# Early attention outputs split from PSUM into the first two token blocks, and token blocks cut at other places

## The chip, the core and the metric

The kernel runs on one core of a Trainium2 chip. TensorE (PE) multiplies matrices; PEld is its weight load. VectorE (DVE), ScalarE (ACT) and GpSimd (POOL) compute elementwise, and SyncE (SP) issues every transfer to or from DRAM. The engines run side by side, each takes its own instructions strictly in the program's order, and semaphores make one wait for another. The metric is the device time of one execution in microseconds.

## The reference

Causal attention with a decay bias, for 4 batches, 8 heads, 576 positions and 64 numbers a head; its output, reshaped to 2304 tokens of 512 numbers, passes through two MoE layers of width 2048. Everything is float32.

```python
scores = np.matmul(q, k.transpose(0, 1, 3, 2)) / np.sqrt(D)
cum = np.cumsum(np.maximum(s, 0.0), axis=-1)
bias = -(cum[:, :, :, None] - cum[:, :, None, :])
scores = np.where(causal, -1e9, scores + np.minimum(bias, 0.0))
attn = np.exp(scores - scores.max(-1, keepdims=True))
x = np.matmul(attn / (attn.sum(-1, keepdims=True) + 1e-09), v)
x = x.transpose(0, 2, 1, 3).reshape(B * S, H * D)
h = x @ w_in                      # first layer
x = (h * np.clip(h + 3.0, 0.0, 6.0) / 6.0) @ w_out
h = x @ w2_in                     # second layer; sp is log(1 + exp(h))
out = (h * np.tanh(sp)) @ w2_out
```

## The kernel before

**Products.** Every MoE operand is split into a high part, rounded to the multiplier's format, and a low part (value minus high part). A product is three matmuls: high by high, high by low, low by high. The split of a weight tile (`load_split`) is six instructions on ACT and DVE.

**Tokens.** The 256 early queries of each batch (`small`, two heads at a time: a pair) become tokens 0 to 1023; the 320 late queries of each batch (`unit`, also in pairs of heads) become tokens 1024 to 2303. `BLOCKS` cuts the tokens into five blocks. A block's tile `blk` holds, for each of 4 chunks of 128 channels, a high and a low part; chunk c comes from head pair c of every batch that the block covers. There are two such tiles (`"blk": 2`), reused in turn.

**MoE.** Each layer walks over the blocks, and in a block over 16 steps (`moe_step`). A step multiplies the 4 chunks by 128 columns of `w_in` (L730, three matmuls a chunk), applies the activation on ACT and DVE (L741, L743, L751), and multiplies by `w_out` (L763 in the first layer, L768 in the second).

**From attention to a block.** A pair's product with v (L683, PV below) is copied from PSUM to a staging tile `st`, stored to a DRAM tile `xs` (L689), and when all stores of a chunk have landed `load_block` loads it into the low half of `blk` (L711) and splits it: a high part (L288, ACT as a rule) and a subtraction (L369, DVE). Late units do the same through L577, L579 and L586. The layers' hand-over goes through `ys` likewise.

**The order.** All instructions are written into a list of nodes with costs, dependencies and priorities. `Plan.run` walks a model of the engines' time and emits each engine's instructions in the order in which the model starts them; the table `T` holds the costs and priorities that set it. Eight small pairs (batches 0 and 1, `FIRST`) come before the MoE; the other eight and the 16 late pairs (`WINDOWS`) are interleaved with the first layer's steps. While that lasts, attention uses two PSUM banks (`units(..., [6, 7], ...)`). `setup_b`, 32 rows for the cumulative sums, uses one `blk` tile first.

Of the kernel before, what the change touches and what calls it, by code (L numbers as in the profile page):

```python
# [10 lines left out]
F32 = mybir.dt.float32  # L11
F32R = mybir.dt.float32r
# [3 lines left out]
ALU = mybir.AluOpType  # L16

NB, NH, S, D = 4, 8, 576, 64
DM, DFF = 512, 2048
P = 128  # L20
NCC = DM // P
NF = DFF // P
NT = NB * S
BLOCKS = [(0, 512), (512, 512), (1024, 256), (1280, 512), (1792, 512)]
NBLK = len(BLOCKS)
# [6 lines left out]
CTOT = sum(CW)  # L32

T = dict(
    sm=4.004, sm2=3.667, w0=5.919, w1=9.193, cum=14.045, wo=1.212, blk0=27.645, blk1=17.49, wo2=34.767,
    wo2r=10.468, win2=5.088, g=13.066, upre=6.773, uhalf=0.799, upost=2.212, uv=0.453, spre=6.03, shalf=0.713,
    spost=1.762, pe=4.858, bias=2.981, la=1, la2=1, wp=5.083, p0=-20.0, p1=2.0, p2=2.856,
    p3=60.483, p4=82.61, p5=145.751, s0=28.447, s1=22.0, s2=22.848, s3=32.154, s4=71.114, s5=32.684,
)
# [27 lines left out]
class Plan:  # L67
# [56 lines left out]
    def run(self):  # L124
# [16 lines left out]
        now = 0.0  # L141
# [81 lines left out]
def v1x(n):  # L223
    return 0.069 + 0.00104 * n
# [19 lines left out]
def tile_attention_moe_moe(ctx, tc, qk1, qk, v1, s, w_in, w_out, w2_in, w2_out, out):  # L244
    nc = tc.nc

    def r(ap):
        return ap.bitcast(F32)
# [34 lines left out]
    def dyn(name):  # L283
        return lambda: pools[name]

    def copy(e, out_, in_):
        if e == "ACT":
            nc.scalar.activation(out=out_, in_=in_, func=AF.Copy)  # L288
        elif e == "POOL":
            nc.gpsimd.tensor_copy(out=out_, in_=in_)  # L290
        else:
            nc.vector.tensor_copy(out=out_, in_=in_)

    setup_b = Buf(main_p, "blk", [P, NCC, 2, 512], F32)

    def rows():
        room = setup_b.t.rearrange("p c a n -> p (c a n)")[0:NB * NH]
        s_sb, one, cum = (room[:, S * i:S * (i + 1)] for i in range(3))
        return s_sb, one, cum, room[:, 3 * S:3 * S + CTOT]
# [114 lines left out]
    class Pair:  # L414
        pass

    xs_n = {(i, c): [] for i in range(NBLK) for c in range(NCC)}
    all_att = []
# [171 lines left out]
    def small(b, h, pair, prio, step, dep0, depc, banks, fi, n_c1, n_id):  # L590
# [66 lines left out]
        n_r = A("DVE", 0.285, recip, n_exp, prio, (), [l])  # L657
        x = Buf(main_p, "st", [P, 512], F32)
        prev_t, n_p = None, []
# [20 lines left out]
        def pv():  # L680
            for g in range(2):
                for c, a in ((0, 0), (1, P)):
                    nc.tensor.matmul(out=po.t[D * g:D * (g + 1), a:N], lhsT=v.t[:, D * (2 * g + c):D * (2 * g + c + 1)], rhs=v.t[:, 4 * D + 384 * g + 2 * a:4 * D + 384 * g + 2 * a + N - a],  # L683
                                     start=c == 0, stop=c == 1)
        n_pv = A("PE", 0.73, pv, n_p + [n_v], post, [po, x], [v])
        pt_nodes.append(n_pv)
        n_x = A(("ACT", "DVE"), (actp(N), v1x(N)), lambda e: copy(e, x.t[:, 0:N], po.t[:, 0:N]), [n_pv], post, (), [po, x])
        i, o = divmod(token(b, 0), 512)
        xs_n[i, h // 2].append(A("SP", 0.5, lambda: nc.sync.dma_start(  # L689
            out=xs[i][h // 2][:, o:o + N], in_=x.t[:, 0:N]), [n_x], post, (), [x], lat=dma(P * N * 4)))  # L690

# [9 lines left out]

    blk, blk_n = {}, {}
    ys_n = {(i, c): [] for i in range(NBLK) for c in range(NCC)}
# [100 lines left out]
    with tc.manual_schedule():  # L804
# [6 lines left out]
        def open_pools():  # L811
# [35 lines left out]
        for n in range(tot):  # L847
            load_wo1(n, pos[n] - T["wo"], [n0])
        for i in range(NBLK):
            load_block(0, i, pos[NF * i] - T["blk0"])  # L850
# [80 lines left out]
```

## Time and profile before

| | us |
|---|---|
| median of three runs | 1023.62 (1021.73 to 1024.51) |
| the profiled execution's own time | 1021.91 |
| its span, first to last instruction | 1020.1 |
| PE busy in it | 988.0 (97%) |
| ACT, DVE busy | 523.1, 523.6 (51% each) |
| mean granted TensorE clock | 0.988 |

The profile is of one execution, 1.71 us below the median of the runs. PE's busy time counts overlapped matmuls once and is not work at full speed: an engine that waits inside a stretch at half clock shows as busy. The pace is read from the chain, where three 512-column matmuls take 0.68 us when they follow each other.

### The profile page before, as it was taken

Reading aid. Unit: us, or ns where it says so; the run is one execution under the profiler, and the core shown is the slowest. Engines: PE = TensorE matmul, PEld = TensorE weight load, DVE = VectorE, ACT = ScalarE, POOL = GpSimd, SP = SyncE. Lnnn points to the kernel's source line nnn. Section 1 sums busy time; section 2 is a strip of 40 time slices with the busy share of each in tenths; the row PEclk is TensorE's granted clock in tenths of the full one; section 3 lists DMA queues with packets and bytes.
Section 4 is the critical chain, followed back from the end, with each engine's and each line's share of the span. In section 5 each row is a group of like instructions: output and inputs, shape, how many; then the busy total and the mean of one; then the engine's idle time right before and its main releaser. Section 6 shows DMA issues by size and latency. Waiting matters only on the chain.

```text
span 1020.1 us, 14027 instructions
## 1 busy us (share of the span) xinstructions
PE 988.0 (97%) x5016; PEld 804.0 (79%) x5016; DVE 523.6 (51%) x1156; ACT 523.1 (51%) x1103; POOL 44.3 (4%) x102
## 2 busy tenths in 40 slices
PE   5789999999999999999999999999999999999998
PEld 3457777778778899978888888888888898888886
DVE  6778889986566666765628898311111212111111
ACT  5887878876655676665426456323222323223222
POOL 2101011200001000000000000000000000000000
PEclk9869999999999999999999999999999999999999
DMA  7778588885566486742646676001000201001001
GB/s 228 247 241 265 204 273 265 283 273 168 162 172 171 143 276 206 243 155 95 234 131 240 226 240 229 22 1 33 30 1 2 82 4 59 1 1 41 1 1 42
DMA packets 60357, 145.02 MB, mean 142 GB/s; under 512 B 6816, under 2 KB 21184, under 8 KB 60288
## 3 DMA queue, kind: packets, MB, share of 16 engines
q1 hardware_dynamic: 60288, 144.12, 43.6%
q8 instruction: 40, 0.66, 0.3%
q14 instruction: 29, 0.24, 0.1%
HBM read 121.32 MB, written 22.78 MB: 141 GB/s over the span
## 4 chain that ended last, share of the span: by engine, by line
PE 89%; ACT 6%; DVE 2%; DMA 2%; issue 1%; SPq 0%; DVEq 0%; ACTq 0%
PE b L730 37%; PE b L768 19%; PE b L763 19%; PE b L489 4%; PE b L573 3%; PE b L535 2%; PE b L628 2%; PE b L683 1%; ACT cb L524 1%; PE b L674 1%; DMA wraw<-in_w_out_dram 1%; ACT pt L288 1%; ACT cb L666 1%; ACT cb L647 1%; ACT wtmp L336 0%
## 5 line engine op out<-in xcount | busy, mean ns | idle before, releaser
L730 PE MATMUL b<-blk,win 128*128 128x512 f32 (+1 forms) x1920 | 498.3, 373 | 2.7 <-DVE blk L369 1.2
L730 PEld LDWEIGHTS b<-blk,win 128*128 128x128 f32 x1920 | 339.6, 189 | 70.0 <-issue 5.2
L763 PE MATMUL b<-g,wo 128*128 128x512 f32 (+1 forms) x960 | 259.7, 379 | 0.1
L763 PEld LDWEIGHTS b<-g,wo 128*128 128x128 f32 x960 | 164.7, 189 | 33.7 <-issue 8.6
L748 ACT ACTIVATE e<-b 128x512 f32<-128x512 f32 (+1 forms) x80 | 44.4, 554 | 254.5 <-PE b L730 254.4
L751 DVE TENSOR_TENSOR g<-e,g 128x512 fp32r<-128x512 f32 (+1 forms) x120 | 76.7, 639 | 173.4 <-ACT g L288 172.3
L768 PE MATMUL b<-wo,wo 128*128 128x512 f32 x432 | 121.1, 390 | 0.0
L768 PE MATMUL b<-wo,g 128*128 128x512 f32 x432 | 121.1, 390 | 0.0
L751 DVE TENSOR_TENSOR wo<-e,wo 128x512 fp32r<-128x512 f32 (+1 forms) x40 | 25.5, 638 | 140.4 <-ACT wo L288 140.3
L768 PEld LDWEIGHTS b<-wo,g 128*128 128x128 f32 x432 | 79.8, 188 | 15.5
L768 PEld LDWEIGHTS b<-wo,wo 128*128 128x128 f32 x432 | 79.8, 188 | 15.4
L741 ACT ACTIVATE e<-b,three 128x512 f32<-128x512 f32 (+1 forms) x80 | 51.2, 643 | 60.2 <-PE b L730 59.7
L288 ACT ACTIVATE g<-e 128x512 fp32r<-128x512 f32 (+1 forms) x108 | 64.1, 594 | 25.3 <-DVE e L743 17.4
L504 ACT ACTIVATE cb<-cb,nm 128x384 f32<-128x384 f32 (+2 forms) x80 | 54.6, 684 | 33.6 <-DVE nm L496 33.4
L743 DVE SCALAR_TENSOR_TENSOR e<-e,b 128x512 f32<-128x512 f32 (+1 forms) x80 | 50.4, 630 | 37.3 <-ACT e L741 36.4
L556 DVE TENSOR_TENSOR pt<-b,pt 128x384 fp32r<-128x384 f32 (+2 forms) x96 | 54.2, 576 | 23.6 <-ACT pt L288 22.4
L288 ACT ACTIVATE pt<-b 128x384 fp32r<-128x384 f32 (+2 forms) x96 | 47.9, 507 | 20.7 <-PE b L535 20.3
L496 DVE CUSTOM_DVE_ANT_0 cb<-b,cb 128x384 f32<-128x384 f32 (+2 forms) x80 | 44.7, 587 | 20.2 <-PE b L489 14.6
L535 PE MATMUL b<-ident,cb 128*128 128x128 f32 x304 | 48.9, 273 | 3.8 <-issue 2.7
L535 PEld LDWEIGHTS b<-ident,cb 128*128 128x128 f32 x304 | 37.3, 140 | 15.7 <-issue 5.6
L573 PEld LDWEIGHTS b<-pt,v 128*128 128x128 f32 x320 | 46.2, 189 | 3.2 <-ACT qk L288 1.2
L336 ACT ACTIVATE wtmp<-wraw 128x512 f32<-128x512 f32 x55 | 36.6, 665 | 23.6 <-DMA wraw<-in_w_out_dram 14.7
(79 smaller groups left out, 877.6 us busy)
## 6 DMA issues: line engine op xcount, KB each, us to landing
wo<-wos SPq DMA_DIRECT2D x64, 512.0 KB, 4.0
wraw<-in_w_in_dram SPq DMA_DIRECT2D x32, 512.0 KB, 4.2
wraw<-in_w_out_dram SPq DMA_DIRECT2D x32, 512.0 KB, 4.5
cb<-cuml SPq DMA_DIRECT2D x16, 896.0 KB, 6.8
wos<-wo SPq DMA_DIRECT2D x16, 512.0 KB, 6.8
qkr<-in_qk_dram SPq DMA_DIRECT2D x16, 480.0 KB, 5.0
qkr<-in_v_dram SPq DMA_DIRECT2D x16, 320.0 KB, 4.3
cb<-cums SPq DMA_DIRECT2D x12, 384.0 KB, 4.9
```

What stands on the lines that cost most here:

```text
L288: nc.scalar.activation(out=out_, in_=in_, func=AF.Copy)
L496: nc.vector.tensor_tensor_reduce(out=p.t[:, o:o + w], in0=pb.t[:, 0:w], in1=cb.t[:, o:o + w], scale=-0.125, scalar=(3.0e38 if a == 0 else ...
L504: nc.scalar.activation(out=p.t[:, o:o + w], in_=p.t[:, o:o + w], func=AF.Exp, scale=-1.0, bias=nm.t[:, k:k + 1], accum_out=l.t[:, k:k + 1],)
L535: nc.tensor.transpose(out=ps.t[:, P * z:P * (z + 1)], in_=p.t[:, o:o + P], identity=ident)
L556: nc.vector.tensor_tensor(out=dl, in0=s_, in1=r(dh), op=ALU.subtract)
L573: nc.tensor.matmul(out=po.t[:, a:nq], lhsT=w, rhs=pt.t[:, k, g, f:f + nq - a], start=c == 0 and k == 0, stop=c == tb - 1 and k == 1)
L730: nc.tensor.matmul(out=hps.t[:, 0:N], lhsT=w.t[:, a, P * c:P * (c + 1)], rhs=x.t[:, c, b, :], start=(c == 0 and k == 0), stop=(c == NCC - ...
L741: a = add("ACT", actp(N, 1), lambda: nc.scalar.activation(out=e0.t[:, 0:N], in_=hps.t[:, 0:N], func=AF.Relu, bias=three, scale=1.0), [prev ...
L743: a = add("DVE", v1x(N), lambda: nc.vector.scalar_tensor_tensor(out=e0.t[:, 0:N], in0=e0.t[:, 0:N], scalar=6.0, in1=hps.t[:, 0:N], op0=ALU ...
L751: gl = add("DVE", v1x(N), lambda: nc.vector.tensor_tensor(out=g.t[:, 1, 0:N], in0=src.t[:, 0:N], in1=r(g.t[:, 0, 0:N]), op=ALU.subtract), ...
L763: nc.tensor.matmul(out=y[j].t[:, 0:N], lhsT=wt.t[:, a, P * j:P * (j + 1)], rhs=g.t[:, b, 0:N], start=(f == 0 and k == 0), stop=(f == NF - ...
L768: nc.tensor.matmul(out=y[j].t, lhsT=g.t[:, a, P * j:P * (j + 1)], rhs=wt.t[:, b, :], start=(f == 0 and k == 0), stop=(f == NF - 1 and k == 2),
```

## The change

`small` writes its output straight into `blk`: the high part is copied from PSUM into `hl(0)`, the low part is subtracted from PSUM by DVE into `hl(1)`. The staging copy, the 16 stores and the 8 loads of the first two blocks are gone, with the 16 splits (8 high parts, 8 subtractions) behind the loads. The two tiles of blocks 0 and 1 are taken at the start, so `setup_b` moves to the attention pool's `pt` tile. Blocks 2, 3 and 4 are 384, 512 and 384 tokens in place of 256, 512 and 512. `Plan.run` multiplies PE's costs by 1.6 in its model's first 60 us, and most numbers of `T` are new.

```diff
-BLOCKS = [(0, 512), (512, 512), (1024, 256), (1280, 512), (1792, 512)]
+BLOCKS = [(0, 512), (512, 512), (1024, 384), (1408, 512), (1920, 384)]
...
-    p3=60.483, p4=82.61, p5=145.751, s0=28.447, s1=22.0, s2=22.848, s3=32.154, s4=71.114, s5=32.684,
+    p3=60.483, p4=83.372, p5=119.475, s0=31.523, s1=22.0, s2=23.277, s3=50.368, s4=66.006, s5=29.106,
...
+                    if e == "PE" and now < 60.0:
+                        c *= 1.6
...
-    setup_b = Buf(main_p, "blk", [P, NCC, 2, 512], F32)
+    setup_b = Buf(dyn("att"), "pt", [P, 3 * S + CTOT], F32)
...
-        x = Buf(main_p, "st", [P, 512], F32)
...
-        n_x = A(("ACT", "DVE"), (actp(N), v1x(N)), lambda e: copy(e, x.t[:, 0:N], po.t[:, 0:N]), [n_pv], post, (), [po, x])
         i, o = divmod(token(b, 0), 512)
-        xs_n[i, h // 2].append(A("SP", 0.5, lambda: nc.sync.dma_start(
-            out=xs[i][h // 2][:, o:o + N], in_=x.t[:, 0:N]), [n_x], post, (), [x], lat=dma(P * N * 4)))
+        c, xb = h // 2, blk[0, i]
+
+        def hl(k):
+            return xb.t[:, c, k, o:o + N]
+        n_xh = A(("ACT", "DVE"), (actp(N), v1x(N)), lambda e: copy(e, hl(0), po.t[:, 0:N]), [n_pv, blk_a[i]], post, (), [po, xb])
+        n_xl = A("DVE", v1x(N), lambda: nc.vector.tensor_tensor(
+            out=hl(1), in0=po.t[:, 0:N], in1=r(hl(0)), op=ALU.subtract), [n_xh], post, (), [po, xb])
+        blk_n[0, i, c] += [n_xh, n_xl]
...
+        for i in range(2):
+            blk[0, i] = Buf(main_p, "blk", [P, NCC, 2, 512], F32R)
+            blk_a[i] = add("X", 0.0, lambda: None, [n0], -1e6, [blk[0, i]])
...
-        for i in range(NBLK):
+        for i in range(2, NBLK):
             load_block(0, i, pos[NF * i] - T["blk0"])
```

The diff shifts the lines: L628, L674, L683, L730, L763 and L369 of before are L631, L676, L685, L736, L769 and L371 of the change, and the new subtraction is L695.

**The first MoE step on PE.** In a row b is a PSUM bank; L674 transposes the normalised scores, L628 makes scores. Before, the step's first chunk stands right behind the eighth pair's PV, and its second and third chunk together ten rows later:

```order
L730 MATMUL b_696<-blk,win 128x512 x3
L674 MATMUL b_713<-ident,cb 128x128 x3
L674 MATMUL b_720<-ident,cb 128x128 x3
L683 MATMUL b_738<-qk 64x256
L683 MATMUL b_738<-qk 64x128
L683 MATMUL b_738<-qk 64x256
L683 MATMUL b_738<-qk 64x128
L628 MATMUL b_746<-qkr 128x128
L628 MATMUL b_746<-qkr 128x256
L628 MATMUL b_756<-qkr 128x128
L628 MATMUL b_756<-qkr 128x256
L730 MATMUL b_696<-blk,win 128x512 x6
```

In the change, the rows that end with the step's fourth chunk are these. The step's first chunk stands ahead of the sixth pair's PV, the second ahead of the seventh's, and the third (in these rows) ahead of the eighth's:

```order
L631 MATMUL b_642<-qkr 128x128
L631 MATMUL b_642<-qkr 128x256
L676 MATMUL b_652<-ident,cb 128x128 x3
L676 MATMUL b_658<-ident,cb 128x128 x3
L736 MATMUL b_569<-blk,win 128x512 x3
L685 MATMUL b_674<-qk 64x256
L685 MATMUL b_674<-qk 64x128
L685 MATMUL b_674<-qk 64x256
L685 MATMUL b_674<-qk 64x128
L631 MATMUL b_687<-qkr 128x128
L631 MATMUL b_687<-qkr 128x256
L736 MATMUL b_569<-blk,win 128x512 x3
```

So the step's twelve matmuls, which before followed the eighth pair's PV with other work between them, now end behind that PV and half a pair of scores.

**SP's queue at the same place.** Before, stores (`xs<-st`) and loads (`blk<-xs`) stand among the loads of weights (`wraw`), inputs (`qkr`, `qk`) and bias rows (`cb`):

```order
L711 DMA blk<-xs_0_74 128x512
L608 DMA qk<-in_v_dram 128x2x128
L689 DMA xs_2_76<-st 128x256
L356 DMA wraw<-in_w_in_dram 128x512
L603 DMA qkr<-in_qk_dram 128x512
L605 DMA cb<-cums 128x768
L711 DMA blk<-xs_1_75 128x512
L608 DMA qk<-in_v_dram 128x2x128
L711 DMA blk<-xs_2_76 128x512
L689 DMA xs_3_77<-st 128x256
L356 DMA wraw<-in_w_in_dram 128x512
L605 DMA cb<-cums 128x768
```

In the change the queue holds only the latter:

```order
L611 DMA qk<-in_v_dram 128x2x128
L358 DMA wraw<-in_w_in_dram 128x512
L606 DMA qkr<-in_qk_dram 128x512
L611 DMA qk<-in_v_dram 128x2x128
L608 DMA cb<-cums 128x768
L606 DMA qkr<-in_qk_dram 128x512
L358 DMA wraw<-in_w_in_dram 128x512
L611 DMA qk<-in_v_dram 128x2x128
L358 DMA wraw<-in_w_in_dram 128x512
L611 DMA qk<-in_v_dram 128x2x128
L608 DMA cb<-cums 128x768
```

Four stores and four loads for block 0, and as many more stores beyond these rows, are gone from it.

**The start of block 2 on PE.** L573 is PV of a late pair, L535 its transposes. Before, the tenth late pair's PV stands between the first two chunks of block 2's first step; block 2 needs the first four late pairs only:

```order
L573 MATMUL b_3789<-pt,v 128x320 x6
L573 MATMUL b_3789<-pt,v 128x192 x2
L573 MATMUL b_3789<-pt,v 128x64 x2
L763 MATMUL b_2566<-g,wo 128x512 x3
L730 MATMUL b_3735<-blk,win 128x256 x3
L535 MATMUL b_3816<-ident,cb 128x128 x3
L763 MATMUL b_2578<-g,wo 128x512 x3
L535 MATMUL b_3828<-ident,cb 128x128 x3
L763 MATMUL b_2536<-g,wo 128x512 x3
L730 MATMUL b_3735<-blk,win 128x256 x3
L763 MATMUL b_2553<-g,wo 128x512 x3
```

In the change, with 384 tokens, block 2 needs late pairs of batches 0 and 1; the last of them is the ninth in the order, and its PV opens these rows (L576). The fourth chunk of block 2's first step stands 13 rows behind the last row here:

```order
L576 MATMUL b_3593<-pt,v 128x320 x6
L576 MATMUL b_3593<-pt,v 128x192 x2
L576 MATMUL b_3593<-pt,v 128x64 x2
L769 MATMUL b_2412<-g,wo 128x512 x3
L538 MATMUL b_3619<-ident,cb 128x128 x3
L769 MATMUL b_2432<-g,wo 128x512 x3
L736 MATMUL b_3631<-blk,win 128x384 x3
L769 MATMUL b_2445<-g,wo 128x512 x3
L538 MATMUL b_3645<-ident,cb 128x128 x3
L769 MATMUL b_2501<-g,wo 128x512 x3
L538 MATMUL b_3656<-ident,cb 128x128 x4
L736 MATMUL b_3631<-blk,win 128x384 x3
```

So the block's first chunk moved to four rows behind the PV of a pair from which its fourth chunk is made.

## Rows read from the trace of the kernel before

**Rows 1.** The page's first part, busy time of each engine.
```profile
PE 988.0 (97%) x5016; PEld 804.0 (79%) x5016; DVE 523.6 (51%) x1156; ACT 523.1 (51%) x1103; POOL 44.3 (4%) x102
```

**Rows 2.** Busy time (x instructions), granted clock, DMA by stretch; columns in the first row.
```profile
core 0: us, PE busy (x) PEld busy (x) DVE busy (x) ACT busy (x) POOL busy (x), PEclk, DMA share, GB/s
...
20.00:57.30 37.30, 26.44 (x150) 16.68 (x146) 27.51 (x109) 32.95 (x112) 5.56 (x10) 0.82 0.76 248
57.30:80.00 22.70, 19.31 (x77) 12.12 (x78) 18.51 (x52) 18.41 (x49) 2.97 (x6) 0.77 0.74 238
...
140.00:215.00 75.00, 72.42 (x384) 55.36 (x383) 69.29 (x160) 62.15 (x137) 8.81 (x14) 1.00 0.77 252
...
490.00:600.00 110.00, 110.00 (x487) 91.10 (x486) 76.18 (x128) 51.56 (x85) 0.00 (x0) 1.00 0.61 207
```

**Rows 3.** Timeline of PE and ACT: start, duration, line, work, idle time before it.
```profile
55.11 1.78 PE L683 MATMUL b<-qk 128*64 128x256 f32 x8
...
57.35 0.49 PE L730 MATMUL b<-blk,win 128*128 128x512 f32 x1 [0.46 <-ACT blk L288]
...
75.30 1.42 PE L730 MATMUL b<-blk,win 128*128 128x512 f32 x5 [0.77 <-DVE blk L369]
...
77.42 0.68 ACT L741 ACTIVATE e<-b,three 128x512 f32<-128x512 f32 x1
```

**Rows 4.** Timeline of SP, the store and the load of block 0's fourth chunk.
```profile
57.95 0.38 SPq L689 DMA_DIRECT2D xs<-st  x1
...
65.02 0.38 SPq L711 DMA_DIRECT2D blk<-xs  x1
```

**Rows 5.** PE's groups by shape, 57.3 to 80 us: count, busy us, mean ns, idle before.
```profile
L730 PE MATMUL b<-blk,win 128*128 128x512 f32 x23 | 8.7, 492 | 2.1 <-DVE blk L369 1.2 <-ACT blk L288 0.9
L674 PE MATMUL b<-ident,cb 128*128 128x128 f32 x18 | 4.3, 352 | 1.3 <-ACT win L288 0.7 <-ACT cb L666 0.4 <-issue 0.3
L628 PE MATMUL b<-qkr 64*128 64x256 f32 x10 | 3.4, 479 | 0.0
...
L683 PE MATMUL b<-qk 128*64 128x256 f32 x8 | 2.4, 533 | 0.0
```

**Rows 6.** Chain that ended last, three places: start, duration, work.
```profile
76.72 0.33 PE b L674 x3
...
80.52 0.85 PE b L628 x4
...
82.26 0.81 PE b L683 x8
...
259.54 0.69 PE b L763 x3
260.23 1.24 PE b L573 x10
261.47 0.77 PE b L763 x3
...
805.72 2.15 PE b L730 x18
```

**Rows 7.** DVE's groups by shape: count, busy us, mean ns.
```profile
L369 DVE TENSOR_TENSOR blk<-blk 128x512 fp32r<-128x512 f32 x32 | 21.7, 686 | 10.0 <-ACT blk L288 9.6
...
L556 DVE TENSOR_TENSOR pt<-b,pt 128x256 fp32r<-128x256 f32 x16 | 6.7, 418 | 0.2
```

**Rows 8.** The columns of rows 2 for a shorter stretch.
```profile
62.00:66.00 4.00, 4.00 (x16) 2.64 (x15) 1.87 (x6) 2.34 (x5) 0.00 (x0) 0.50 0.80 214
```

**Rows 9.** Timeline of DVE, a late pair's last add and the split behind it, twice.
```profile
438.06 0.49 DVE L579 TENSOR_TENSOR st<-b,st 64x320 f32<-64x320 f32 x1 [0.99 <-ACT st L577]
...
447.49 0.69 DVE L369 TENSOR_TENSOR blk<-blk 128x512 fp32r<-128x512 f32 x1
...
218.13 0.49 DVE L579 TENSOR_TENSOR st<-b,st 64x320 f32<-64x320 f32 x1
...
236.95 0.42 DVE L369 TENSOR_TENSOR blk<-blk 128x256 fp32r<-128x256 f32 x1
```

More of the change, by code (lines that the diff above doesn't have):

```diff
@@ L34 @@
 T = dict(
-    sm=4.004, sm2=3.667, w0=5.919, w1=9.193, cum=14.045, wo=1.212, blk0=27.645, blk1=17.49, wo2=34.767,
-    wo2r=10.468, win2=5.088, g=13.066, upre=6.773, uhalf=0.799, upost=2.212, uv=0.453, spre=6.03, shalf=0.713,
-    spost=1.762, pe=4.858, bias=2.981, la=1, la2=1, wp=5.083, p0=-20.0, p1=2.0, p2=2.856,
-    p3=60.483, p4=82.61, p5=145.751, s0=28.447, s1=22.0, s2=22.848, s3=32.154, s4=71.114, s5=32.684,
+    sm=4.004, sm2=3.667, w0=5.919, w1=9.193, cum=14.045, wo=0.795, blk0=27.645, blk1=17.49, wo2=40.913,
+    wo2r=11.978, win2=5.088, g=29.605, upre=6.511, uhalf=0.883, upost=2.212, uv=0.304, spre=9.559, shalf=0.728,
+    spost=1.761, pe=4.796, bias=2.278, la=1, la2=1, wp=5.083, p0=-8.796, p1=2.0, p2=2.856,
+    p3=60.483, p4=83.372, p5=119.475, s0=31.523, s1=22.0, s2=23.277, s3=50.368, s4=66.006, s5=29.106,
 )
@@ L292, in copy @@
             nc.vector.tensor_copy(out=out_, in_=in_)
-    setup_b = Buf(main_p, "blk", [P, NCC, 2, 512], F32)
+    setup_b = Buf(dyn("att"), "pt", [P, 3 * S + CTOT], F32)
     def rows():
-        room = setup_b.t.rearrange("p c a n -> p (c a n)")[0:NB * NH]
+        room = setup_b.t[0:NB * NH]
         s_sb, one, cum = (room[:, S * i:S * (i + 1)] for i in range(3))
@@ L415, in tile_attention_moe_moe @@
         pass
+    blk, blk_n, blk_a = {}, {}, {}
     xs_n = {(i, c): [] for i in range(NBLK) for c in range(NCC)}
@@ L684, in pv @@
                                      start=c == 0, stop=c == 1)
-        n_pv = A("PE", 0.73, pv, n_p + [n_v], post, [po, x], [v])
+        n_pv = A("PE", 0.73, pv, n_p + [n_v], post, [po], [v])
         pt_nodes.append(n_pv)
-        n_x = A(("ACT", "DVE"), (actp(N), v1x(N)), lambda e: copy(e, x.t[:, 0:N], po.t[:, 0:N]), [n_pv], post, (), [po, x])
         i, o = divmod(token(b, 0), 512)
-        xs_n[i, h // 2].append(A("SP", 0.5, lambda: nc.sync.dma_start(
-            out=xs[i][h // 2][:, o:o + N], in_=x.t[:, 0:N]), [n_x], post, (), [x], lat=dma(P * N * 4)))
+        c, xb = h // 2, blk[0, i]
[5 more added lines that the diff above has]
+        blk_n[0, i, c] += [n_xh, n_xl]
     def units(b, ta, tb, prio, step, n0, nc0, banks, fi=False, hs=(0, NH)):
@@ L700, in units @@
         all_att.extend(pl.nodes[n1:])
-    blk, blk_n = {}, {}
     ys_n = {(i, c): [] for i in range(NBLK) for c in range(NCC)}
@@ L825, in tile_attention_moe_moe @@
                   lat=dma(NB * NH * 1500 * 4))
+        for i in range(2):
+            blk[0, i] = Buf(main_p, "blk", [P, NCC, 2, 512], F32R)
+            blk_a[i] = add("X", 0.0, lambda: None, [n0], -1e6, [blk[0, i]])
+            for c in range(NCC):
+                blk_n[0, i, c] = []
         all8 = [6, 7, 4, 5, 0, 1, 2, 3]
```

## The prediction

> **What bounds the kernel now.** I read the page's first part, the busy times by stretch, the timeline around the first MoE step, the groups by shape, and the chain that ended last, in this order. PE is busy 97% of the span, ACT and DVE half of it [rows 1]. By stretch, PE is full from 80 us on: between 490 and 600 us it is busy for 110.00 of 110 us, and even from 140 to 215 us, where DVE is at 92%, it idles 2.6 of 75 us [rows 2]. So the matmuls are a floor that this change doesn't lower, and time can only come from what PE loses. It loses most at the start: from 20 to 57.3 us it is busy 26.44 of 37.3 us at a clock of 0.82, while ACT is at 88%; the small pairs are made there, and ACT and DVE set their pace.
>
> The place that the change touches is behind that. The eighth pair's PV ends at 56.9 us; the first step's first matmul starts at 57.35, its last two only at 75.30, and its activation at 77.42 [rows 3]. What the step waits for is the way through DRAM: the fourth chunk's store was issued at 57.95, its load at 65.02 [rows 4], and the matmuls at 75.30 waited for DVE's split of it [rows 3].
>
> What PE loses there comes from counting its work at full-clock pace. Between 57.3 and 80 us stand 23 MoE matmuls, 18 transposes, 10 wide scores (and 10 narrow) and 8 wide PVs (and 8 narrow) [rows 5]. In the chain three MoE matmuls take 0.69 us, three transposes 0.33, four score records 0.85, eight PV records 0.81 [rows 6]. That is 23 x 0.23 + 6 x 0.33 + 5 x 0.85 + 2 x 0.81 = 13.1 us. The stretch is 22.7 us long, so 9.6 us are lost, to waits and to the half clock that rows show from 62 to 66 us [rows 8].
>
> **The change, part by part.** The sum is made against the profiled execution's 1021.9 us; the runs' median lies 1.7 higher, and the forecast is given on the median's scale. Less than 0.3% (3.1 us) can't be told from no change here.
>
> *Until the eighth pair's output is split: +0.6.* In the order, DVE has 157 instructions up to that subtraction, where it had done 141 by 57.3 us: 8 subtractions, one more weight tile, some normalisations taken from ACT. ACT has 90 against 96. Ten more at the 0.42 us of a 256-column subtraction [rows 7] are 4.2 us; ACT and DVE together worked 60.5 us in the 37.3 us before [rows 2], 1.62 us per us, so 2.6 us later. By then PE has nine MoE matmuls behind it that it had not before, with the same scores, transposes and PVs: 9 x 0.23 = 2.0 earned. Bounds: -2.0 (DVE, idle a quarter of that stretch, hides all) to +2.1 (all ten instructions on the path). I take the joint pace, since ACT's 88% leaves little room.
>
> *The stretch behind it: -6.1.* The step then lacks only three matmuls, and up to the fourth step nothing but weight tiles that the order puts earlier. What stays lost in such a stretch: PE idles 2.6 in 75 us from 140 to 215 us [rows 2], so 0.7 in 20 us. A return from attention to the MoE costs 0.08 (three matmuls take 0.77 behind a PV, 0.69 otherwise [rows 6]), ten of them 0.8. And the clock: a stretch of 4 us at half [rows 8] costs 2.0; before, half clock lasted longer, but behind PE's pauses. 9.6 - 3.5 = 6.1. Bounds: 0 gained (ACT and DVE take the place of the wait) to 8.8 (only the returns stay).
>
> *More returns: +0.9.* The order has 215 returns from attention to the MoE, before 196. Without four ahead of the first step's end and ten in the stretch above, and six of before's until 80 us, it is 201 against 190: 11 x 0.08. The shortest gap taken, 0 is the other bound.
>
> *Block 2's last chunk: +0.5.* Block 2 now needs the ninth late pair, whose PV stands just ahead of it. From that PV to the block's fourth chunk the order has 24 MoE matmuls of 512 columns, 9 of 384, 19 transposes, one PV and six returns: 24 x 0.23 + 9 x 0.173 + 19 x 0.11 + 1.24 + 0.5 = 10.9 us of cover [rows 6]. What must fit in it is a copy and an add, a store, a load and a split. Seven late pairs between 350 and 490 us show that chain; in the middle one 9.6 us pass from the add's end (438.55) to the split's (448.18) [rows 9], and the copy and the add itself need some 1.1 before. So cover and chain are equal: usually no wait, now and then 1 or 2. Behind PE's wait stand all its matmuls. The longest case, at 218 us, took 18.8 us [rows 9], where nothing was in a hurry: 0 to 9 are the bounds, and 0.5 is near the lower since the seven are the nearer rows.
>
> The Trainium skill has a shorter chain: DMA: Bandwidth & Descriptors, section "Anatomy of one DMA", gives a transfer a fixed 2 us and its bytes at 436 GB/s. By that, estimated for a store of 32 KB and a load of 192 KB, the two take 4.6 us, the cover holds in every case, and the sum below would be 0.5 us lower. That section fits transfers issued from GpSimd; these are issued by SP, and here 8.9 us lie between the middle case's add and its split's start.
>
> *Blocks of 384: 0.* Both kernels have the same columns and matmuls. A 256-column matmul takes 2.15/18 = 0.119 us, a 512-column one 0.23 [rows 6]. On the line through both, two of 384 cost just what a 256 and a 512 do. In proportion to the 512 it would be -2.3 us over 576 triples, in proportion to the 256 +4.6; 384 is midway, so I take the line.
>
> *Hidden.* DVE's 16 subtractions of 256 columns instead of 8 of 512 cost 16 x 0.418 - 8 x 0.686 = 1.2 us more [rows 7], half of it counted above, the rest while PE is full. A pair's bank is held a subtraction longer, 8 x 0.42 = 3.3 us if every later pair stalled PE; the second bank covers it. SP issues 24 transfers less, and waits for nobody's pace in doing so. Block 1's tile is free from the start, but its first matmul stands 350 MoE matmuls behind. The sums' rows leave `pt` long before a late pair takes it. The first layer's last block is a quarter shorter, with the second layer's weights split beside it; DVE at 76.18 of 110 us there [rows 2] would rise to 92%: hidden, barely.
>
> Sum: 0.6 - 6.1 + 0.9 + 0.5 = -4.1, so 1017.8, and 1019.5 on the median's scale.
>
> **The rivals.**
> - *DVE takes the place of the wait.* It carries 57 instructions more than before in the whole program (ACT 57 fewer), and is at 92% from 140 to 215 us [rows 2]; if PE now waits for weight tiles and activations from 60 us on, the 6.1 are not gained: +2.0, 1025.6, no change. For it: the matmuls' floor leaves DVE less room when PE comes earlier. Against it: by the order, DVE's work up to the same step is no larger, and before it kept pace with a full PE.
> - *More than forecast.* The step comes while the clock is up, PE waits for nothing, and DVE's idle quarter hides its added work: -2.0 - 8.8 + 0.9 = -9.9, 1013.7. For it: the new order feeds PE MoE matmuls between the pairs, where it paused. Against: weights are still made by the same two engines.
> - *Slower: block 2's last chunk comes late.* The store stands in SP's in-order queue, the splits in ACT's and DVE's. With the chain of 218 us PE waits 18.8 + 1.1 - 10.9 = 9.0 us: -4.1 - 0.5 + 9.0 = +4.4, 1028.0. It makes the kernel slower by more than 0.3% from a chain of 18.4 us on. For it: the new place has no slack. Against: the seven nearer chains.
>
> That the transfers are not gone is no rival: the order shows SP's queue without them.
>
> **How the numbers follow.** The forecast (1016.5 to 1022) has 0.42, "more" 0.21, DVE 0.22, block 2 0.15. The time is the forecast's, 1019.5. Faster by over 0.3% is below 1020.5: seven tenths of the forecast and all of "more", 0.50. Slower is block 2 and a little of DVE's case, 0.17; the rest, 0.33, is within 0.3%. The range goes from 1012, below "more" with a 384-column gain, to 1027, past DVE's case and up to most of block 2's; some 0.15 is left out.
>
> **What would show it.** Right: the first activation starts near 62 us instead of 77.4; from there to 80 us PE loses 3 to 4 us against its work; no store or load of `xs` before the late pairs'; 384-column matmuls at 0.17 us; no wait above 1 us at block 2's fourth chunk. Wrong: the eighth pair's subtraction later than 63 us; PE waiting for `win`, `wo` or `g` between 60 and 215 us; a wait of several us for `blk` when the 384-column matmuls begin; or a wait where the second layer begins.

## The result, and the profile after

| | before | after |
|---|---|---|
| median (lowest to highest), us | 1023.66 (1021.73 to 1024.51) | 1013.81 (1013.02 to 1014.32) |
| the profiled execution, us | 1021.91 | 1013.87 |
| its span, us | 1020.1 | 1012.1 |

The ratio is 0.9902, 95% interval 0.9885 to 0.9919: faster, by 9.85 us, where 4.1 were forecast. The profiled executions differ by 8.0 us, since that of before lay 1.7 below its median; the stretches below are theirs.

The page's first line of the change, against [rows 1]: DVE has 57 instructions more, ACT 57 fewer, and PE the same 5016.

```profile
PE 992.1 (98%) x5016; PEld 826.6 (82%) x5016; DVE 541.8 (54%) x1213; ACT 496.0 (49%) x1046; POOL 45.0 (4%) x102
```

Busy time by stretch in the change, with the columns of [rows 2]:

```profile
20.00:57.30 37.30, 33.39 (x174) 20.01 (x171) 32.13 (x122) 32.80 (x107) 5.15 (x11) 0.91 0.69 217
57.30:80.00 22.70, 22.49 (x94) 15.24 (x95) 19.66 (x54) 16.64 (x45) 4.03 (x6) 0.85 0.71 221
140.00:215.00 75.00, 74.16 (x404) 58.49 (x403) 66.59 (x155) 55.21 (x125) 7.22 (x16) 1.00 0.78 247
490.00:600.00 110.00, 110.00 (x561) 100.54 (x560) 70.80 (x122) 49.55 (x85) 0.00 (x0) 1.00 0.61 208
...
58.50:65.20 6.70, 6.70 (x17) 4.17 (x16) 5.79 (x20) 4.94 (x15) 0.00 (x0) 0.50 0.59 182
```

From 20 to 57.3 us PE ran 174 matmuls where it had run 150, and it idled 0.8 us from 140 to 215 us in place of 2.6. It still ran at half clock from 58.5 to 65.2 us.

The change's timeline at the first step, to be read beside [rows 3]:

```profile
45.93 0.96 PE L736 MATMUL b<-blk,win 128*128 128x512 f32 x3
...
48.47 1.19 PE L736 MATMUL b<-blk,win 128*128 128x512 f32 x3
...
52.70 1.27 PE L736 MATMUL b<-blk,win 128*128 128x512 f32 x3 [0.40 <-ACT blk L290]
...
56.63 0.49 PE L736 MATMUL b<-blk,win 128*128 128x512 f32 x1 [0.72 <-ACT blk L290]
57.51 0.73 PE L736 MATMUL b<-blk,win 128*128 128x512 f32 x2 [0.39 <-DVE blk L695]
...
57.04 0.42 DVE L695 TENSOR_TENSOR blk<-b,blk 128x256 fp32r<-128x256 f32 x1
...
59.12 0.67 ACT L747 ACTIVATE e<-b,three 128x512 f32<-128x512 f32 x1
```

The four chunks are multiplied while the pairs are still being made, the last of them right behind its own subtraction, and the activation starts at 59.12 us in place of 77.42.

**Where the time went.** PE's busy time hides slow matmuls, so I count its work instead. Each matmul is given the time that it takes in an undisturbed run of its kind (0.227 us for 512 columns, 0.173 for 384, 0.119 for 256, 0.108 for a transpose; small scores and PVs by [rows 6], and so on). The whole program then is 940.7 us in every kernel here. Time passed minus the work that PE had started is *lost time*. What is lost in each stretch, in the profiled execution of every run of this study (the experiments below say what each run is):

| us lost | to 57.3 | 57.3 to 80 | 80 to 490 | 490 to end | sum |
|---|---|---|---|---|---|
| before | 29.0 | 10.4 | 35.2 | 4.7 | 79.3 |
| after | 26.9 | 5.6 | 29.9 | 9.0 | 71.3 |
| split_alone | 27.9 | 3.5 | 35.3 | 4.7 | 71.5 |
| no_split | 31.1 | 11.8 | 29.9 | 9.5 | 82.3 |
| old_blocks | 26.8 | 6.9 | 40.2 | 4.8 | 78.6 |
| no_factor | 32.4 | 3.2 | 36.3 | 9.0 | 81.0 |
| old_table | 28.4 | 2.8 | 33.3 | 9.0 | 73.5 |
| nudged | 26.3 | 6.2 | 33.0 | 9.0 | 74.4 |
| dve_twice | 27.2 | 7.8 | 31.3 | 8.9 | 75.3 |
| act_twice | 26.6 | 7.9 | 29.8 | 9.0 | 73.3 |
| split_factor | 28.0 | 2.6 | 35.2 | 4.8 | 70.5 |
| old_blocks_p5 | 26.8 | 7.0 | 27.9 | 4.7 | 66.4 |
| old_blocks_p5_163 | 26.6 | 5.7 | 28.5 | 4.7 | 65.5 |
| searched | 26.3 | 4.8 | 27.9 | 4.7 | 63.7 |
| no_split_p5 | 31.3 | 11.9 | 30.9 | 5.1 | 79.3 |
| no_factor_p5 | 31.2 | 4.3 | 34.9 | 4.7 | 75.0 |

Each row is one execution, and the executions of one kernel differ (no_factor took 1016.38 to 1024.08 us, and its profiled one 1023.54), so that a difference of a us between two rows says little.

From before to after: -2.1, -4.7, -5.4, +4.2, together -8.0 (worked out before rounding). The forecast had looked for its gain in the second column alone; what the last two columns hold, which nearly cancels, was not in it.

The rows of the third column's stretch, before and then after:

```profile
80.00:490.00 410.00, 404.26 (x2344) 329.69 (x2343) 295.48 (x685) 285.20 (x616) 31.16 (x72) 1.00 0.66 210
```

```profile
80.00:490.00 410.00, 407.56 (x2279) 336.52 (x2278) 309.45 (x717) 267.59 (x577) 30.76 (x73) 1.00 0.64 203
```

PE's open idle time fell from 5.7 to 2.4 us, and between these two kernels nearly all of that is one group of waits. PE's transposes of late pairs, 80 to 490 us, before and after (the last fields are idle time before them and what ended it):

```profile
L535 PE MATMUL b<-ident,cb 128*128 128x128 f32 x304 | 48.9, 273 | 3.8 <-issue 2.7 <-DVE pt L556 0.8
```

```profile
L538 PE MATMUL b<-ident,cb 128*128 128x128 f32 x304 | 48.7, 273 | 0.6 <-DVE pt L559 0.4
```

3.2 of the 5.4 us are here; the other 2.2 are in matmuls that follow each other more closely, and what closed them up is not shown. One such wait of before, in its timeline:

```profile
208.97 1.03 PE L535 MATMUL b<-ident,cb 128*128 128x128 f32 x8
...
209.17 0.63 ACT L288 ACTIVATE g<-e 128x512 fp32r<-128x512 f32 x1 [0.80 <-PE b L763]
209.71 1.06 ACT L288 ACTIVATE pt<-b 128x512 fp32r<-128x512 f32 x2
210.32 1.29 DVE L556 TENSOR_TENSOR pt<-b,pt 128x512 fp32r<-128x512 f32 x2 [0.22 <-ACT pt L288]
...
211.11 1.09 PE L535 MATMUL b<-ident,cb 128*128 128x128 f32 x5 [1.11 <-issue]
```

Eight transposes fill the two banks that attention has. Their copies out of PSUM stand on ACT behind a split of `g`, which waits for PE itself; PE goes on when they and DVE's subtractions have emptied the banks. Where such a knot falls is a matter of the written order.

The fourth column has two parts. The chain of the change in the second layer, in a block of 384 tokens (start, duration, work), and at the same place that of the run "split_alone", whose blocks are the old ones:

```profile
839.26 0.70 PE b L774 x3
839.96 0.53 PE b L736 x3
840.49 0.69 PE b L774 x3
841.18 0.52 PE b L736 x3
```

```profile
839.54 0.68 PE b L772 x3
840.22 0.68 PE b L734 x3
```

Three matmuls of 384 columns take 0.52 to 0.53 us, on the forecast's line or just above it; but three of 512 between them take 0.69 to 0.70 in place of 0.68. The kernel before has the same surcharge in its one block of 256 tokens, in its chain:

```profile
799.78 0.69 PE b L768 x3
800.47 0.35 PE b L730 x3
800.83 0.69 PE b L768 x3
```

The change has two blocks of 384 tokens, in place of that one and one of 512. From 490 to 1000 us it loses about 3 us more than before, nearly all of it in matmuls whose neighbours have another width. And at the end, in the timeline of before and then of the change:

```profile
1009.78 2.88 PE L768 MATMUL b<-wo,wo 128*128 128x512 f32 x12
```

```profile
1003.62 0.86 PE L774 MATMUL b<-wo,wo 128*128 128x512 f32 x3
1004.91 2.47 PE L774 MATMUL b<-wo,g 128*128 128x512 f32 x9 [0.44 <-ACT g L290]
```

Before, twelve matmuls stood behind the last ones with the input weights and covered the last activation. In the change, whose last block has three groups of output where it had four, only three stand there, and PE waits: 1.0 us lost.

### The profile page after: what moved, and what is told of

Same layout as the page of the kernel before. It is cut to its first block, busy times and chain, and to the rows that moved or that the text cites. A ratio compares the mean times of both kernels' runs of the same rounds, so it can differ in the third digit from the quotient of the medians.

```text
span 1012.1 us, 13938 instructions
## 1 busy us (share of the span) xinstructions
PE 992.1 (98%) x5016; PEld 826.6 (82%) x5016; DVE 541.8 (54%) x1213; ACT 496.0 (49%) x1046; POOL 45.0 (4%) x102
## 4 chain that ended last, share of the span: by engine, by line
PE 89%; DVE 2%; DMA 2%; ACT 2%; issue 0%; DVEq 0%; ACTq 0%; SPq 0%
PE b L736 38%; PE b L774 20%; PE b L769 19%; PE b L492 4%; PE b L576 3%; PE b L538 3%; PE b L631 1%; DMA ys<-st 1%; PE b L685 1%; PE b L676 1%; DMA xs<-st 0%; ACT cb L527 0%; DVE pt L559 0%; DMA blk<-xs 0%; DMA cb<-cums 0%
## 5 line engine op out<-in xcount | busy, mean ns | idle before, releaser
L736 PE MATMUL b<-blk,win 128*128 128x512 f32 (+1 forms) x1920 | 504.4, 374 | 2.8 <-DVE e L749 1.2
L736 PEld LDWEIGHTS b<-blk,win 128*128 128x128 f32 x1920 | 348.9, 189 | 61.8 <-issue 5.7
L769 PE MATMUL b<-g,wo 128*128 128x512 f32 (+1 forms) x960 | 259.1, 380 | 0.1
L769 PEld LDWEIGHTS b<-g,wo 128*128 128x128 f32 x960 | 168.5, 188 | 27.8 <-issue 10.5
L290 ACT ACTIVATE g<-e 128x512 fp32r<-128x512 f32 (+1 forms) x103 | 60.5, 587 | 65.6 <-PE b L769 52.5
L749 DVE SCALAR_TENSOR_TENSOR e<-e,b 128x512 f32<-128x512 f32 (+1 forms) x80 | 50.4, 630 | 19.0 <-ACT e L747 18.6
L576 PEld LDWEIGHTS b<-pt,v 128*128 128x128 f32 x320 | 46.8, 189 | 1.7
L492 PE MATMUL b<-qk 64*128 64x384 f32 (+2 forms) x288 | 46.5, 364 | 0.6 <-DVE pt L559 0.6
```

What stands on the lines that cost most here:

```text
L492: nc.tensor.matmul(out=ps[g].t[:, 0:w], lhsT=t.t[s_, ka, qo:qo + P], rhs=t.t[s_, kb, nk0 + a:nk0 + e], start=k == 0, stop=k == 2)
L576: nc.tensor.matmul(out=po.t[:, a:nq], lhsT=w, rhs=pt.t[:, k, g, f:f + nq - a], start=c == 0 and k == 0, stop=c == tb - 1 and k == 1)
L736: nc.tensor.matmul(out=hps.t[:, 0:N], lhsT=w.t[:, a, P * c:P * (c + 1)], rhs=x.t[:, c, b, :], start=(c == 0 and k == 0), stop=(c == NCC - ...
L749: a = add("DVE", v1x(N), lambda: nc.vector.scalar_tensor_tensor(out=e0.t[:, 0:N], in0=e0.t[:, 0:N], scalar=6.0, in1=hps.t[:, 0:N], op0=ALU ...
L769: nc.tensor.matmul(out=y[j].t[:, 0:N], lhsT=wt.t[:, a, P * j:P * (j + 1)], rhs=g.t[:, b, 0:N], start=(f == 0 and k == 0), stop=(f == NF - ...
```

## The experiments

Theory A: the split's way past DRAM is the gain. Theory B: the written order is. The planner runs anew for every run, so that each of them but 7 and 8 has an order of its own, split_alone too.

**1 to 4: the parts apart.**

split_alone: before, with the diff of `small`, `setup_b`, the early `blk` tiles and `load_block` only.

```diff
...
+        n_xl = A("DVE", v1x(N), lambda: nc.vector.tensor_tensor(
+            out=hl(1), in0=po.t[:, 0:N], in1=r(hl(0)), op=ALU.subtract), [n_xh], post, (), [po, xb])
...
-        for i in range(NBLK):
+        for i in range(2, NBLK):
```

> The kernel before with the direct split alone: blocks, table of costs and priorities, and PE's cost in the planner are the old ones. Theory A (the way through DRAM was the loss): the first activation comes near 60 us in place of 77.4, and most of the 9.85 us is there: 1015 to 1018 us. Theory B (the written order is the gain: PE filled between the pairs, fewer waits until 490 us): the split alone gives what the stretch from 57.3 to 80 us gave at most, and loses some of it to an order nobody adjusted: 1019 to 1023 us.

Measured 1012.99 us, ratio 0.9893 (0.9874 to 0.9912): the whole gain, and more than Theory A gave it. Its rows for 57.3 to 80 us and its first activation:

```profile
57.30:80.00 22.70, 21.35 (x110) 14.92 (x108) 20.59 (x55) 20.28 (x58) 3.45 (x6) 1.00 0.65 217
```

```profile
62.13 0.67 ACT L745 ACTIVATE e<-b,three 128x512 f32<-128x512 f32 x1
```

110 matmuls where before had 77 and the change 94, at full clock: 6.9 us less lost there than before. From 80 to 490 us it loses what before does, 35.3.

no_split: the same lines taken out of the change.

```diff
...
-        for i in range(2, NBLK):
+        for i in range(NBLK):
```

> The changed kernel with the staging copy, store, load and split of blocks 0 and 1 put back; new blocks, new table and PE's factor of 1.6 stay. Theory A: the activation is late again (75 us or more), 57.3 to 80 us loses again about 5 us more than in the change: 1019 to 1025 us. Theory B: the order alone keeps at least half of the 9.85 us: 1014 to 1018 us.

Measured 1025.33 us, 1.0012 (0.9994 to 1.0031): no gain left, Theory A (0.3 above the end of its range). Its timeline and its stretch:

```profile
77.89 1.73 PE L676 MATMUL b<-ident,cb 128*128 128x128 f32 x6 [3.11 <-DMA cb<-cuml]
79.27 2.81 PE L732 MATMUL b<-blk,win 128*128 128x512 f32 x6
...
80.94 0.69 ACT L743 ACTIVATE e<-b,three 128x512 f32<-128x512 f32 x1 [0.79 <-PE b L732]
```

```profile
57.30:80.00 22.70, 17.89 (x73) 10.89 (x74) 18.53 (x52) 18.76 (x52) 2.58 (x7) 0.66 0.90 275
```

The DMA engines are at 0.90, against 0.71 in the change, and a load of bias rows is late as well. Yet from 80 to 490 us it loses only 29.9, like the change: Theory B has something too, in another stretch.

old_blocks: `BLOCKS` of before in the change.

```diff
-BLOCKS = [(0, 512), (512, 512), (1024, 384), (1408, 512), (1920, 384)]
+BLOCKS = [(0, 512), (512, 512), (1024, 256), (1280, 512), (1792, 512)]
```

> The changed kernel with blocks of 512, 512, 256, 512, 512 tokens again; direct split, new table and factor stay. Theory M (a 384-column triple beside a 512-column one costs more than each alone, and the smaller last block leaves the last activation uncovered): from 490 us to the end the change lost about 3.3 us on the first and 1.0 on the second against before; both come back, 1008.5 to 1011 us, unless the table, made for other blocks, loses in the first half. Rival (384 is on the line, as forecast, and the new blocks help the first layer): 1013 to 1017 us.

Measured 1020.85 us, 0.9971 (0.9956 to 0.9985). It is outside both ranges; only Theory M's "unless", a table made for other blocks, had named it. Behind 490 us the 4.2 us are back, as Theory M says; but 80 to 490 us lose 40.2, at one place:

```profile
415.90 0.94 PE L736 MATMUL b<-blk,win 128*128 128x512 f32 x3
432.94 2.38 PE L736 MATMUL b<-blk,win 128*128 128x512 f32 x4 [1.49 <-DVE blk L294]
...
424.00 0.80 SPq L589 DMA_DIRECT2D xs<-st  x2
...
429.65 0.32 SPq L717 DMA_DIRECT2D blk<-xs  x1
```

The fourth chunk of the block from token 1280 is stored at 424.00 and loaded at 429.65. The new table puts batch 3's late pairs among batch 2's; this block, cut at the old place, needs the last of batch 2's earlier. Around it PE also runs at half clock:

```profile
427.00:437.00 10.00, 7.80 (x22) 5.54 (x23) 4.95 (x17) 4.94 (x11) 0.00 (x0) 0.50 0.22 64
```

It is the forecast's third rival, a chunk that comes late, at another block and in another kernel.

no_factor: the change without the two lines of PE's factor.

```diff
-                    if e == "PE" and now < 60.0:
-                        c *= 1.6
```

> The changed kernel without PE's factor of 1.6 in the planner's first 60 us. If the factor puts the MoE matmuls between the pairs, where PE waited, taking it out brings back waits of 2 us each before 57.3 us and some 2 to 4 us in time: 1016 to 1018 us. If the direct split alone does that, nothing changes: 1013 to 1015 us.

Measured 1020.75 us, 0.9967 (0.9948 to 0.9987), 7 us more than the change, in place of 2 to 4. The waits between the pairs are back:

```profile
24.07 1.51 PE L674 MATMUL b<-ident,cb 128*128 128x128 f32 x6 [3.22 <-issue]
...
34.22 1.13 PE L674 MATMUL b<-ident,cb 128*128 128x128 f32 x6 [2.16 <-ACT cb L666]
...
49.09 1.04 PE L674 MATMUL b<-ident,cb 128*128 128x128 f32 x3 [1.21 <-issue]
```

5.5 us more are lost until 57.3 us than in the change, 2.4 fewer up to 80, and 6.4 more from 80 to 490, where no cost was changed, only the order that followed. The profiled execution lies 2.8 us above the median, and some of the 6.4 is clock: it was 0.50 from 81.2 to 84.4 us.

**5 and 6: is the gain behind 80 us the order's?** old_table has `T` of before in the change; nudged ends the factor at 55 us of the model's time.

```diff
...
-    p3=60.483, p4=83.372, p5=119.475, s0=31.523, s1=22.0, s2=23.277, s3=50.368, s4=66.006, s5=29.106,
+    p3=60.483, p4=82.61, p5=145.751, s0=28.447, s1=22.0, s2=22.848, s3=32.154, s4=71.114, s5=32.684,
```

```diff
-                    if e == "PE" and now < 60.0:
+                    if e == "PE" and now < 55.0:
```

> The changed kernel with the old table of costs and priorities; split, blocks and factor stay. Theory T (the 5.4 us that the change loses less from 80 to 490 us are fewer waits of transposes behind ACT and DVE, and belong to the written order that the new table makes): without it the stretch loses some 35 us against its work again, as before, in place of 29.9, and the 384-column blocks still cost 4.2 behind it: 1017 to 1021 us. Rival (fewer transfers, copies and splits give those 5.4 us, whatever the table): 1013 to 1015 us.

> The changed kernel with the factor of 1.6 on PE's modelled cost only until 55 us of the model's time in place of 60; about an eighth of PE's rows change places, all behind the first step. Theory T: the waits of transposes come at other places and in another number; the stretch from 80 to 490 us loses 30 to 36 us where the change loses 29.9, and the time is 1014 to 1020 us. Rival: the order is sturdy and the gain is the split's: 29 to 31 us lost there, 1013 to 1014.5 us.

Measured 1018.96 (0.9939, 0.9917 to 0.9961) and 1016.91 (0.9922, 0.9907 to 0.9937). 80 to 490 us lose 33.3 and 33.0 (the profiled execution of old_table is the fastest of its four, 1016.01). Times and losses are Theory T's: five of the model's microseconds took 3 of the 5.4 back. Its waits are so only in part. PE's open idle time in the stretch is 4.5 and 4.7 us, against 2.4 in the change, but before transposes of late pairs it is 2.7 us in old_table and this in nudged:

```profile
L538 PE MATMUL b<-ident,cb 128*128 128x128 f32 x304 | 48.5, 273 | 1.0 <-DVE pt L559 0.8
```

split_alone, with the old table, has 0.8 there and loses 35.3. So the gain is the order's, and the knots of transposes are where it showed between before and after, not its general cause.

**7 and 8: what paces the small pairs.** The order stays the same to the row; one instruction of each of the first eight pairs runs twice.

```diff
-        n_xl = A("DVE", v1x(N), lambda: nc.vector.tensor_tensor(
-            out=hl(1), in0=po.t[:, 0:N], in1=r(hl(0)), op=ALU.subtract), [n_xh], post, (), [po, xb])
+        n_xl = A("DVE", v1x(N), lambda: [nc.vector.tensor_tensor(
+            out=hl(1), in0=po.t[:, 0:N], in1=r(hl(0)), op=ALU.subtract) for _ in range(2 if fi else 1)], [n_xh], post, (), [po, xb])
```

```diff
-        n_xh = A(("ACT", "DVE"), (actp(N), v1x(N)), lambda e: copy(e, hl(0), po.t[:, 0:N]), [n_pv, blk_a[i]], post, (), [po, xb])
+        n_xh = A(("ACT", "DVE"), (actp(N), v1x(N)), lambda e: [copy(e, hl(0), po.t[:, 0:N]) for _ in range(2 if fi else 1)], [n_pv, blk_a[i]], post, (), [po, xb])
```

> The changed kernel with the subtraction of each of the first eight pairs executed twice, into the same place; the order is the same to the row. Eight more DVE instructions of 0.42 us, 3.3 us of DVE work before the first activation. If DVE's idle part hides them: first activation at 59 to 59.7 us as in the change (59.1), 1013.5 to 1014.5 us. If ACT and DVE set the pace together, as the forecast's first term took it (3.3 us at 1.7 us of work per us): first activation near 61 us, 1015.5 to 1016.5 us.

> The changed kernel with the copy of the high part of each of the first eight pairs executed twice on ACT; the order is the same to the row. Eight more ACT instructions of 0.37 us, 2.9 us of ACT work before the first activation. If ACT alone sets the pace of the small pairs: first activation near 62 us, 1016 to 1017 us. If it has room (88% busy): first activation before 60 us, 1013.5 to 1014.5 us.

Measured 1017.11 (1013.23 to 1017.83) and 1015.11 (1014.30 to 1016.28), against 1013.81. The first activation, with DVE's and then with ACT's instruction doubled, stands in their timelines at

```profile
60.76 0.67 ACT L747 ACTIVATE e<-b,three 128x512 f32<-128x512 f32 x1
```

```profile
59.80 0.67 ACT L747 ACTIVATE e<-b,three 128x512 f32<-128x512 f32 x1
```

so 1.64 later for 3.3 us of DVE work, 0.68 later for 2.9 us of ACT work. DVE's idle part hides half, ACT's three quarters. Each time lies 0.6 us above the range that the text had given with such an activation. Up to 80 us both lose 2.0 to 2.5 us more than the change, and both stay at half clock for longer: from 58.5 to 68.5 us these rows show 0.50 for either, where the change is at full clock from 65.3 on (DVE's first, then ACT's):

```profile
58.50:68.50 10.00, 9.35 (x23) 5.96 (x24) 8.42 (x26) 5.45 (x15) 0.07 (x1) 0.50 0.55 188
```

```profile
58.50:68.50 10.00, 10.00 (x25) 6.41 (x25) 7.51 (x24) 6.27 (x18) 0.00 (x0) 0.50 0.55 189
```

Half clock for 3.3 us longer is an estimated 1.6 us, so most of the cost in these executions can be the clock's. It did not come each time: one of dve_twice's four executions had a mean clock of 0.997, where the others had 0.990 and 0.991, and took 1013.23 us.

**9 to 12: the old blocks with a table that suits them.** The change with the old blocks, and of the table only `p5`, the place of batch 3's late pairs (163.0 in the second run); "searched" moves ten numbers of it (p5 to 163.0, p3 to 57.1, the rest by 4 to 17%).

```diff
...
-    p3=60.483, p4=83.372, p5=119.475, s0=31.523, s1=22.0, s2=23.277, s3=50.368, s4=66.006, s5=29.106,
+    p3=60.483, p4=83.372, p5=145.751, s0=31.523, s1=22.0, s2=23.277, s3=50.368, s4=66.006, s5=29.106,
```

The fourth is split_alone with the factor.

```diff
+                    if e == "PE" and now < 60.0:
+                        c *= 1.6
```

> The changed kernel with the old blocks, as the run with old blocks and the new table, but with one number of the table set back: the late pairs of batch 3 get the priority 145.751 of before in place of 119.475. There the fourth chunk of the block from 1280 to 1791 came 17 us late (its first step's matmul at 432.94 us, the step's third at 415.9), since batch 3's pairs stood among batch 2's, which that block needs. Theory M (blocks of 384 cost 4.2 us from 490 us on; the rest of the old-block run's loss is this one chunk): no wait there, nothing lost behind 490 us, 1008.5 to 1011 us, faster than the change and than the split alone. Rival (the old blocks cost as much in the first layer as they give behind it): 1012 to 1016 us.

> As the run with priority 145.751, with 163: batch 3's late pairs begin later still. Theory M: the same 1008.5 to 1011 us, unless the last block's chunks now come late (a wait of several us at 450 to 475 us). Rival: 1012 to 1016 us.

> The changed kernel with the old blocks and a table in which several numbers were moved until the planner's own model gave the shortest end, 2.2 us below the one with priority 145.751. If the model's differences of 2 us hold on the chip: 1007 to 1009 us. If they are below what the model can tell: 1008.5 to 1013 us, not to be told from the neighbours.

> The kernel before with the direct split and PE's factor of 1.6, old table and blocks. The split alone took 1013.0. If the factor alone fills PE between the small pairs, it loses 1 to 2 us less until 57.3 us than the split alone: 1011 to 1013 us. If the order behind it is changed only by chance: 1011 to 1018 us, with the difference between 80 and 490 us.

Measured 1008.86 (0.985, 0.9821 to 0.9878), 1008.00 (0.9843, 0.9809 to 0.9877), 1006.24 (0.9821, 0.9789 to 0.9853) and, for the split with the factor on the old table, 1012.68 (0.989, 0.986 to 0.992). One number undoes the late chunk, and three versions beat both kernels: Theory M (the second run 0.5 below its range), with 27.9 to 28.5 us lost from 80 to 490 and 4.7 behind. Against old_blocks the first loses 12.3 us less from 80 to 490: 6.2 are open idle time (1.33 us against 7.49), and most of the rest is, by an estimate, the half of the 10 us that old_blocks spent at half clock. "searched" fell below even its first range; until 80 us it loses 31.1, the two neighbours 33.8 and 32.3. The factor on the old table changes nothing: its worth is that of the table made with it.

**13 and 14: the order without the split, and without the factor.** The run with `p5=145.751` again, with the edit of no_split and of no_factor.

```diff
...
-        for i in range(2, NBLK):
+        for i in range(NBLK):
```

```diff
-                    if e == "PE" and now < 60.0:
-                        c *= 1.6
```

> The fastest plain combination so far (direct split, old blocks, factor, new table with priority 145.751; 1008.9 us) with the way of blocks 0 and 1 through DRAM put back. If the split is worth about 8 us under either order, and the order about 5 on its own: some 8 to 12 us more, 1016 to 1021 us, with the first activation again behind 75 us. If the order is only good because the split made room for it, nothing is left of it: 1022 to 1027 us.

> The same combination without the factor of 1.6. On the old table the factor moved the time from 1013.0 to 1012.7 only; on the new table with the new blocks its absence cost 7 us. If that cost belongs to the pair of table and factor: 1012 to 1017 us. If it came with the blocks of 384: 1008 to 1010 us.

Measured 1022.71 (0.9984, 0.9963 to 1.0005) and 1017.59 (0.995, 0.9936 to 0.9963). The first falls into the range of "nothing is left", but not for that text's reason. Without the split, 30.9 us are lost from 80 to 490, against 35.2 before: that part of the order's gain needs no split. But 43.2 are lost by 80 us, 9.4 more than with the split and 3.8 more than before: a table made for early chunks is worse than the old one when they come late. The split is worth 11 us under the old order (1012.99 against 1024.19 for before beside it) and 14 under this one. Without the factor, 7.0 us more are lost from 80 to 490, at the same blocks: its cost belongs to the pair of table and factor, as the first text said, though the time is 0.6 above its range.

## Why the prediction was right and wrong

**The direction was right, the size was not**; and the number of the rival "more than forecast", 1013.7, is nearly the measured one, by luck. That rival put all its gain ahead of 80 us, with the clock up; the change was at half clock from 58.5 to 65.2 us, and 5.4 of its gain came later, and 4.2 were lost again behind that. Between the profiled executions the four parts of the sum came to -2.1, -4.7, -5.4 and +4.2, where +0.6, -6.1, +1.4 and 0 were put.

**Until the eighth pair's output is split (+0.6): mis-sized, -2.1.** The subtraction ended at 57.46 us, 0.2 behind the mark, where 2.6 were forecast. At a fixed order the method holds for DVE alone: 1.64 us later for 3.3 us of DVE work (dve_twice) is near the 2.0 that 1.62 us of work per us gives, but 0.68 for 2.9 us of ACT work (act_twice) is far below the 1.8 that it gives there. What failed is a joint pace, taken over into another order. In the change ACT and DVE worked 64.93 us in the 37.3, 1.74 per us: they stood idle for less of it. The split alone stayed at 59.93 and first activated at 62.13, close to the "near 62" of the forecast, with -1.1 in this column.

**The stretch behind it (-6.1): right in kind, -4.7.** The activation came 18 us earlier, and no store or load of `xs` was left there. The change lost 5.6 where 3.5 were put, and half clock, 6.7 us and not 4, is an estimated 1.35 of the difference. The 4 us were the width of the window of [rows 8], not a length that was read: before's clock was 0.50 from 59.7 to 69.8 us. The split alone, without half clock there, lost the 3.5 although 2.0 of them had been put for the clock; that the sum fits it is luck.

**More returns (+0.9) and block 2's last chunk (+0.5): the step that failed.** From 80 to 490 us the change lost 5.4 us less, where these two terms made it lose 1.4 more. The sentence behind it was "PE is full from 80 us on", so that only more returns and one late chunk were looked for there. It took busy time for work: 35.2 us were lost there before, more than three times the 10.4 of the stretch that I worked on, 5.7 of them open idle time (PE busy 404.26 of 410 us). The new table and the factor were read at two places only, and their effect behind 80 us was set to the count of returns. The change and six runs that keep the factor and the new table, but for `p5`, show 27.9 to 31.3 there, with the split or without (old_blocks, with its late chunk, apart); before and the six with either of them missing or moved show 33.0 to 36.3. PE's open idle time parts them too: 1.2 to 3.6 us against 4.4 to 5.7. Half clock has a part in it, an estimated half us of loss for each us: there are 3 to 7 us of it in this stretch in split_alone, split_factor, no_factor and no_factor_p5, 2 and 4 us in the two runs without the split, and none in before, old_table, nudged and the change. Block 2's last chunk itself came in time. Its way through DRAM and its first matmuls in the change's timeline (the last row is the fourth chunk of the block's first step, right behind a PV):

```profile
332.23 0.49 DVE L582 TENSOR_TENSOR st<-b,st 64x320 f32<-64x320 f32 x1 [0.38 <-ACT st L580]
...
332.76 0.79 SPq L589 DMA_DIRECT2D xs<-st  x2
335.63 0.32 SPq L717 DMA_DIRECT2D blk<-xs  x1
...
339.51 0.55 DVE L371 TENSOR_TENSOR blk<-blk 128x384 fp32r<-128x384 f32 x1
...
339.71 1.40 PE L576 MATMUL b<-pt,v 128*128 128x320 f32 x10
340.94 0.78 PE L736 MATMUL b<-blk,win 128*128 128x384 f32 x3
```

From the add's end (332.72) to the split's (340.06) the chain took 7.3 us, where 9.6 were put; PE came 0.9 us after it and did not wait. The Trainium skill's rule (DMA: Bandwidth & Descriptors, "Anatomy of one DMA"), by which I had estimated 4.6 us for the two transfers (the terms add up to 4.5), would have put 0 on this term, as measured. Its time for the transfers does not agree with the trace: the 32 KB store landed 2.8 us and the 192 KB load 3.2 us after its issue, 6.0 together.

**Blocks of 384 (0): wrong, +4.2.** Their own pace is on the line that I took, 0.173 to 0.177 us. I had priced them alone, not beside 512, though the chain of before shows 0.69 for three beside 256, and had not looked at what covers the last activation. Every run with 384 loses 8.9 to 9.5 behind 490 us, every run without 4.7 to 5.1.

**Hidden** were, as forecast, the banks held longer, SP's queue and `pt`; PE does not wait for the second layer's weights. DVE, forecast at 92% from 490 to 600 us, was busy for 70.80 of the 110 us.

**Smaller slips** that moved nothing: the 384-column matmuls are 1152, so 384 triples and not 576, and the chain from which the kernel is slower by 0.3% is 18.6 us with the copy and the add, not 18.4.

So the split is the gain, the new order is a second one of 5 us behind 80 us, and the new blocks give most of that back. That the net equals the split alone is a coincidence of the two. Two things remain open. No run parts the split's shorter way from the transfers, copies and splits that it saves. And no run shows why PE waits less in this order; that it is this order and not a rule, the nudge shows.

## What to carry to other kernels

Price a re-planned order by what PE loses in every stretch, as time minus work, not by its busy share: 57.3 to 80 us stood out, but from 80 to 490 us three times as much was lost. Take a table of priorities, its cost factors and the block boundaries as one thing; one number of it was worth 12 us when the blocks moved back. When a change bundles several edits, run them apart: here the first alone was as fast as all, and all but the new blocks, with one number adjusted, was 5 us faster.

## What the runs showed of the hardware

Matmuls of 512 columns that alternate with matmuls of 384 or of 256 take 0.69 to 0.70 us for three, in place of 0.68 among themselves (after, before and split_alone). And in the profiled executions of dve_twice and act_twice, 0.7 to 1.6 us of delay at the first step went with 2.0 to 2.5 us lost by 80 us, and with half clock shown to 68.5 us in place of 65.2.
